# Moving the norm's roots and row scaling of the coming couple to VectorE, inside the visit

## The chip, the cores and the metric

The kernel runs on one core of one Trainium2 chip. The metric is the device time of one execution in microseconds (us), as the median of several runs. A core has several engines that run their own queues of instructions side by side: TensorE (PE in the profile, with PEld for its weight loads), VectorE (DVE), ScalarE (ACT), GpSimd (POOL) and SyncE (SP, which here issues the DMAs). An engine takes its instructions in order: one that waits holds up all that is queued behind it.

## The reference

An attention block with normalised queries and keys feeds a two-layer feed-forward block. In the notation of the reference:

```
q, k, v: (8, 12, 448, 64)      w_in: (768, 2048)      w_out: (2048, 768)
rmsnorm(x, g) = x / sqrt(mean(x*x, axis=-1) + 1e-6) * g
q_n, k_n = rmsnorm(q, g_q), rmsnorm(k, g_k)
attn = softmax(q_n @ k_n^T / 8)
x = (attn @ v).transpose(0, 2, 1, 3).reshape(3584, 768)
h = x @ w_in;  out = (h * sigmoid(h)) @ w_out
```

All inputs and outputs are fp32. The step that the change touches is the norm of the rows of q and k: the mean of the squares of 64 elements, its reciprocal square root, and the multiplication of each row by it.

## The kernel before, in words

The 96 heads are worked off in 24 *couples* of four heads, three couples to a batch. For each couple c the main loop calls `visit(c)` (L1366) and then `between(c)` (L1431). From couple 6 on (GROUP is 6) the rows of q and k lie in a layout of quarters, 32 wide, and are normalised before they are transposed. What the change touches applies from there on.

**The norm of one couple** has these steps.

- `sum_squares` (L649): ScalarE squares the 128x896 rows of q or of k (L654), VectorE sums each 32 of them (L655) into `rms`, 28 columns for q and 28 for k.
- `scale` (L660): TensorE multiplies the sums by a matrix called `ident` (L667), which adds the two halves of a row. The product lands in a tile named "sc". There are two such PSUM buffers, and the tiles of the scores use the same two. VectorE reads the tile (L668) and makes the reciprocal root by a start value and three Newton steps (L672 to L681; small instructions of 128x56). Then GpSimd multiplies the rows by the factors (L689), once for q and once for k, 128x896 each.
- `flip` (L633): VectorE transposes blocks of 32 of q (L636) or k (L639), and the loads of the next rows into the freed place are issued on SP (L251; eight DMAs for each of q and k). `gain` (L643) multiplies the transposed keys by g_q and g_k on ScalarE.

**A visit** (L1366) is TensorE's work on scores and on weighted sums of v in a fixed order: `scores(c, j, i)` (L701) multiplies into one "sc" tile, and ScalarE takes the exponential of it (L715); `weigh` (L725) adds the products with v into two PSUM banks, "av0" and "av1". The last products of couple c−1 are made at the start of visit(c). `turn` (L720) copies one column into such a bank (L723) before TensorE goes on in the other order of halves; in turn(1) this copy is made by VectorE from couple 6 on. When the products of couple c−1 are complete, `divide` (L802) multiplies them by the reciprocal sums on VectorE (L805). In the visits of couples 12 and 18 `sum_x` (L944) follows, with sums of x for the feed-forward products (L828), and in those of couples 7 to 10 sums or roundings of the weights w_in (`weights_in_visit`, L1356). Two or more adds of exponentials (`add`, L752, L761) end the visit.

**Between two visits** (L1431) TensorE works on the feed-forward products x @ w_in. They are made by a scheme of seven products for each 2x2 block (L859 on), of HW = 3 steps of multiplication each per half (six matmul records of a full array, 2.25 us). VectorE adds finished products to earlier ones (L831), ScalarE copies others (L881, L891), and GpSimd adds some (L893). The product tiles use two PSUM buffers named "mm". `fill` (L1305) deals these steps out: it takes steps until the share of this call is used up, calls the entries of `others` spread evenly over these steps, and the entries of `prompt` one at the start and one after each finished product. Each couple has two such calls. The first carries the late adds, the weights' roundings and sums, and the squares of the keys of couple c+2; the second carries the reciprocals of the couple's sums of exponentials in two halves (L790; L781 are TensorE's sums), `gain`, and the squares of the queries of couple c+2. The second half of the reciprocals issues six DMAs on SP that spread them over partitions (`spread`, L796 and L798); `divide` of the next visit needs them. Before the change, `flip` of the queries of c+1 stands at the start of `between`, `flip` of the keys of c+1 between TensorE's last sum and the first reciprocal, and `scale(c + 2)` at the very end of `between(c)`. There are exceptions at the start: the keys of couple 6 are scaled at the end of between(4), behind `pair_up` (L691), which fills `ident` by copies on GpSimd (L695); the queries of couple 6 in visit(5); couple 7 at the start of between(6).

Which of two buffers a tile gets is decided when the program is built. The order of each engine's instructions is the order in which the program issues them.

After couple 23 the remaining feed-forward products (L1180, L1217) follow, from about 778 us to the end. The change does not touch them.

Of the kernel before, what the change touches and what calls it, by code (L numbers as in the profile page):

```python
# [11 lines left out]
F32 = mybir.dt.float32  # L12
AF = mybir.ActivationFunctionType
ALU = mybir.AluOpType
# [15 lines left out]
BANK = 512  # L30
# [487 lines left out]
def bounded(  # L518
# [114 lines left out]
    def flip(c, name):  # L633

        if name == "q":
            nc.vector.transpose(qT.rearrange("p i s -> p (i s)"), q_of(c)[:, 0 : z.NK])  # L636
            load_q(c + 1)
            return
        nc.vector.transpose(kT, place[f"k{c % 2}"])  # L639
        if c + 2 < NC:  # L640
            loads["k"](c + 2)
# [15 lines left out]
            in_=squares.rearrange("p (n e) -> p n e", e=z.Q), axis=AX.X, op=ALU.add,  # L657
        )

    def scale(c, names="qk"):  # L660

        if c >= NC:
            return
        start = "qk".index(names[0]) * n
        f = norm.rms[c % 2][:, ds(start, len(names) * n)]
        t = ps.tile([P, 2, BANK], F32, name="sc", bufs=2)[:, 0, 0 : len(names) * n]
        nc.tensor.matmul(t, ident, f, start=True, stop=True)  # L667
        nc.vector.tensor_scalar(  # L668
            out=f, in0=t, scalar1=1.0 / D, scalar2=1e-6, op0=ALU.mult, op1=ALU.add
        )  # L670
        y, a = (squares[:, ts(i, len(names) * n)] for i in range(2))
        nc.vector.tensor_scalar(  # L672
            out=y.bitcast(I32), in0=f.bitcast(I32), scalar1=-0.5, scalar2=RSQRT_START,
            op0=ALU.mult, op1=ALU.add,
        )
        for i in range(3):
            nc.vector.tensor_tensor(out=a, in0=f, in1=y, op=ALU.mult)
            nc.vector.scalar_tensor_tensor(
                out=a, in0=a, scalar=-0.5, in1=y, op0=ALU.mult, op1=ALU.mult
            )  # L680
            nc.vector.scalar_tensor_tensor(  # L681
                out=f if i == 2 else y, in0=a, scalar=1.5, in1=y, op0=ALU.add, op1=ALU.mult
            )
        for i, name in enumerate(names):
            rows = q_of(c)[:, 0 : z.NK] if name == "q" else place[f"k{c % 2}"]
            rows = rows.rearrange("p (n e) -> p n e", e=z.Q)
            factor = f[:, ts(i, n)]
            factor = factor.rearrange("p (n one) -> p n one", one=1).to_broadcast([P, n, z.Q])
            nc.gpsimd.tensor_tensor(out=rows, in0=rows, in1=factor, op=ALU.mult)  # L689

    def pair_up():  # L691

# [27 lines left out]
    def turn(step, copy):  # L720

        if step != weighed["step"]:
            copy(banks[1][:, S : S + 1], minus_half)  # L723
# [581 lines left out]
    def fill(others=(), prompt=()):  # L1305


        others, prompt, steps, dealt = list(others), list(prompt), 0, 0
        if prompt:
            prompt.pop(0)()  # L1310
        filler["due"] += filler["share"]
        total = max(1, int(filler["due"] / S))
        while filler["due"] > 0:
            step = next(filler["work"], None)
            if step is None:
                break
            filler["due"] -= step
            steps += 1
            if prompt and steps % HW == 0:
                prompt.pop(0)()  # L1320
            while dealt < min(len(others), len(others) * steps // total):
                others[dealt]()
                dealt += 1
        filler["due"] = min(filler["due"], 0.0)
        for other in prompt + others[dealt:]:
            other()
# [24 lines left out]
    def weights_in(c, half):  # L1351
        i = 2 * (c - GROUP) + half
        work = [step_of[step] for step in ("ro" if c < GROUP else halves.get(i, ""))]
        return work + [lambda a=a: sum_w_in(*a) for a in sums_halves.get(i, ())]
# [11 lines left out]
    def visit(c):  # L1366

        if c < GROUP - 1:
            beside = normalise(c + 1)
        elif c <= GROUP:  # L1370
            beside = [lambda: sum_squares(c + 1, "q")]
        else:
            beside = []
        if c < NC:
            scores(c, 0, 0)
        run_all(beside[0:1])
        if c > 0:
            weigh(c - 1, LEFT)
            weigh(c - 1, LEFT - 1, 0)
            turn(1, nc.scalar.copy if c < GROUP else nc.vector.tensor_copy)  # L1380
        if c < NC:
            scores(c, 0, 1)
        if c == 0:
            run_all(beside[1:2])
        if c > 0:
            weigh(c - 1, LEFT - 1, 1)
            if c - 1 < EARLY:
                for i in range(2):
                    nc.vector.tensor_copy(x_of(c - 1, i), sums[i])
                run_all(beside[1:2])  # L1390
                if inverting:
                    if c > 1:
                        divide(c - 2, None)
                    run_all(inverting)
                    inverting.clear()
            else:
                divide(c - 1, sums)
                run_all(beside[1:2])
                if c < NC and c % GROUP == 0:
                    for i in range(0 if c == GROUP else 1, HW):  # L1400
                        sum_x(last_two(c), i)
                weights_in_visit(c)
            if c + 1 < NC:
                loads["vrest"](c + 1)
        if c == NC:
            return
        if c == GROUP - 1:
            scale(c + 1, "q")
        scores(c, 1, 0)
        scores(c, 1, 1)  # L1410
        if c < GROUP:
            run_all(beside[2:3])
        weigh(c, 0, 1)
        scores(c, 2, 0)
        weigh(c, 1, 1)
        turn(0, nc.scalar.copy)
        if c < GROUP:
            run_all(beside[3:4])
        scores(c, 2, 1)
        weigh(c, 0, 0)  # L1420
        run_all(add(c, 1))
        weigh(c, 1, 0)
        scores(c, LEFT)
        if c + 1 < NC:
            loads["v"](c + 1)

    def run_all(work):
        for piece in work:
            piece()

    def between(c):  # L1431

        def transposes_and_sums():
            summing = sum_up(c)
            if c < GROUP:
                next(summing)
            if c == GROUP:
                flip(c + 1, "q")
            if c < GROUP - 1:
                transpose_k(c + 1)  # L1440
            elif c < NC - 1:
                flip(c + 1, "k")
            reciprocals = next(summing)
            if GROUP - 1 <= c < NC - 1:
                reciprocals.insert(2, gain)
            if GROUP // 2 <= c <= EARLY:
                divide(c - 1, None)
            return reciprocals

        if c < GROUP - 1:  # L1450
            transpose_q(c + 1)
        elif c == GROUP:
            scale(c + 1)
        elif c < NC - 1:
            flip(c + 1, "q")
        if c < GROUP // 2:
            inverting.extend(transposes_and_sums())
        elif c == GROUP - 1:
            run_all(transposes_and_sums())
        if c >= GROUP and c % GROUP == 0:  # L1460
            fetched = range(AHEAD) if c == GROUP else ()
            columns = products - 2 * HW * S * len(fetched)
            work = halves_in(last_two(c), range(HF), plain_in, dict(begun), fetched)
            begin(work, columns, 2 * GROUP)
            begun.clear()
        late = add(c, LEFT - 1) + add(c, LEFT) if c >= GROUP else []
        keys = [lambda: sum_squares(c + 2, "k")] if c >= GROUP - 2 else []
        queries = [lambda: sum_squares(c + 2, "q")] if c >= GROUP else []
        fill(late + weights_in(c, 0) + keys)
        prompt = transposes_and_sums() if GROUP // 2 <= c != GROUP - 1 else []  # L1470
        if c == GROUP // 2:
            begin(make_ahead([0, 1]), AHEAD * 2 * HW * S, GROUP - 1)
        fill(weights_in(c, 1), prompt + queries)
        if c == GROUP - 2:
            pair_up()
            scale(c + 2, "k")
        elif c >= GROUP:
            scale(c + 2)
        if c % GROUP == GROUP - 1:
            finish()  # L1480
            if c == GROUP - 1:
                begun[0] = fetch_ahead([0, 1], 0)
            else:
                sum_x([c // GROUP * 2, c // GROUP * 2 + 1], 0)
        if GROUP <= c < NC - 1:

            nc.scalar.activation(first, minus_half, AF.Exp)
        if c == NC - 1:
            while rounder.load():
                pass  # L1490
# [236 lines left out]
```

## Time and profile before

| what | value |
|---|---|
| median of 3 runs | 1362.72 us (1362.27 to 1364.60) |
| the profiled execution | 1364.28 us, of it the span 1362.5 us |
| TensorE's granted clock, mean | 0.989 of full speed |
| ScalarE's exponentials L715 (128x448) | 542 ns each, 252 of them |
| VectorE's reductions L655 | 1082 ns each, 36 of them |
| VectorE's reciprocals L790 | 1533 ns each, 36 of them |
| feed-forward products L873 | 549 ns a matmul record, busy 258.6 + 187.2 us in the two largest groups |

A line of the profile's groups names the source line, the engine, the operation, output and inputs, the shape, how many there were, then the busy time and the mean of one, and at last the engine's idle time just before them with what ended most of it. Busy time of TensorE includes that of instructions that overlap in its pipeline: a matmul record of 549 ns starts every 375 ns when nothing holds it up. In a timeline a line is start, busy time, engine, source line, operation, count; in square brackets stands the idle time before it and what released it.

### The profile page before, as it was taken

To read this page: it belongs to the slowest core of one execution; us is meant where nothing else is said; L and a number is where in the kernel's file an instruction comes from. 1 tells how busy PE (TensorE), PEld (TensorE's weight loads), DVE (VectorE), ACT (ScalarE), POOL (GpSimd) and SP (SyncE) were. 2 spreads that over 40 slices of the span, in tenths; PEclk is the share of its full clock that TensorE was granted. 3 is DMA by queue.
4 is the path that set the end of the run, shared out by engine and by line. 5 is a ranking of instruction groups with operands and counts; after the bars stand their busy time and mean duration, and the time that the engine had idled before them with its cause. 6 is when DMAs were issued, how large, how long until landed. Compare 5 with 4: busy or idle time off the path is not lost.

```text
span 1362.5 us, 19714 instructions
## 1 busy us (share of the span) xinstructions
PE 1302.9 (96%) x7113; PEld 818.6 (60%) x7113; DVE 991.2 (73%) x1785; ACT 475.7 (35%) x859; POOL 266.2 (20%) x205
## 2 busy tenths in 40 slices
PE   8997898999899999899999999999999999999998
PEld 4333343444344444344444455556999999999998
DVE  5786987886756656765664677679887787878786
ACT  7875364464344544444454234420010000000000
POOL 5762223331122122111210134420000000000000
PEclk9999899999999999899999999999999999999999
DMA  8564355334333333233331247531413232323311
GB/s 234 149 151 99 88 147 143 94 75 105 79 78 78 92 92 79 84 78 79 78 92 45 99 134 245 179 118 43 128 50 122 74 97 74 102 78 99 111 60 38
DMA packets 252559, 139.43 MB, mean 102 GB/s; under 512 B 190436, under 2 KB 236388, under 8 KB 252452
## 3 DMA queue, kind: packets, MB, share of 16 engines
q1 hardware_dynamic: 251888, 137.09, 36.1%
q8 instruction: 58, 0.95, 0.3%
q0 software_dynamic: 256, 0.79, 0.2%
q14 instruction: 49, 0.40, 0.1%
q10 hardware_dynamic: 308, 0.20, 0.1%
HBM read 88.47 MB, written 41.29 MB: 95 GB/s over the span
## 4 chain that ended last, share of the span: by engine, by line
PE 64%; DVE 2%; DMA 1%; SPq 1%; ACT 1%; issue 0%; POOL 0%; ACTq 0%; DVEq 0%; POOLq 0%
PE alone L1180 22%; PE mm L873 17%; PE mm L1180 7%; PE alone L873 7%; PE sc L710 4%; PE av L747 4%; PE alone L1217 2%; PE mm L1217 1%; PE sc L781 1%; DVE sums_x L828 0%; DMA hidden<-stage 0%; SPq L251 0%; DVE work L831 0%; DMA work<-work 0%; POOL parts L893 0%
## 5 line engine op out<-in xcount | busy, mean ns | idle before, releaser
L873 PE MATMUL mm<-x,W 128*128 128x448 f32 x636 | 258.6, 549 | 13.8 <-ACT stage L891 5.2
L873 PEld LDWEIGHTS mm<-x,W 128*128 128x128 f32 x636 | 117.6, 191 | 147.5 <-issue 111.9
L873 PE MATMUL mm<-sums_x,W 128*128 128x448 f32 x456 | 187.2, 549 | 7.4 <-DVE stage L831 4.4
L747 PE MATMUL av<-work,rows 64*64 64x448 f32 x1296 | 152.1, 552 | 20.9 <-DVE av L723 15.4
L710 PE MATMUL sc<-work 64*64 64x448 f32 x1344 | 163.7, 558 | 2.2 <-ACT work L715 2.0
L761 DVE TENSOR_TENSOR work<-work 128x896 f32<-128x896 f32 (+1 forms) x114 | 128.6, 1153 | 51.1 <-PE av L747 46.0
L715 ACT ACTIVATE work<-sc 128x448 f32<-128x448 f32 x252 | 120.8, 542 | 95.5 <-PE sc L710 85.6
L873 PEld LDWEIGHTS mm<-sums_x,W 128*128 128x128 f32 x456 | 84.9, 191 | 102.3 <-issue 80.9
L1180 PE MATMUL alone<-W,rows 128*128 128x192 f32 x608 | 113.0, 326 | 0.0
L747 PEld LDWEIGHTS av<-work,rows 64*64 64x64 f32 x1296 | 53.0, 135 | 98.2 <-issue 39.4
L893 POOL TENSOR_TENSOR parts<-parts,stage 128x448 f32<-128x448 f32 x31 | 41.5, 1340 | 318.5 <-DVE parts L831 290.1
L1180 PEld LDWEIGHTS alone<-W,rows 128*128 128x128 f32 x608 | 101.2, 190 | 0.0
L710 PEld LDWEIGHTS sc<-work 64*64 64x64 f32 x1344 | 51.9, 136 | 76.3 <-issue 36.5
L689 POOL TENSOR_TENSOR rows<-rows,rms 128x896 f32<-128x896 f32 x36 | 62.7, 1762 | 143.9 <-ACT work L715 49.2
L505 POOL DMA_DIRECT2D out_dram<-x x2 | 1.3, 652 | 443.1 <-DVE x L831 443.1
L1011 ACT ACTIVATE stage<-stage 128x896 f32<-128x896 f32 x63 | 57.3, 945 | 44.6 <-DVE stage L831 43.9
L1180 PE MATMUL alone<-W,work 128*128 128x192 f32 x382 | 72.2, 326 | 0.0
L1180 PEld LDWEIGHTS alone<-W,work 128*128 128x128 f32 x382 | 63.8, 190 | 0.0
L655 DVE TENSOR_REDUCE rms<-rows 128x28 f32<-128x896 f32 x36 | 38.9, 1082 | 31.8 <-ACT rows L654 31.7
L881 ACT COPY stage<-mm 128x448 f32<-128x448 f32 x27 | 14.3, 531 | 130.2 <-PE mm L873 130.1
L1190 ACT COPY rows<-alone 128x192 f32<-128x192 f32 x34 | 10.8, 318 | 137.5 <-PE alone L1180 79.0
L790 DVE RECIPROCAL work<-sc 128x224 f32<-128x224 f32 x36 | 55.1, 1533 | 1.0 <-PE sc L781 1.0
(248 smaller groups left out, 2168.0 us busy)
## 6 DMA issues: line engine op xcount, KB each, us to landing
hidden<-stage SPq DMA_DIRECT2D x63, 448.0 KB, 2.8
work<-hidden SPq DMA_DIRECT2D x21, 1024.0 KB, 5.2
rows<-in_moe_w_out_dram SPq DMA_DIRECT2D x32, 384.0 KB, 3.4
W<-in_moe_w_in_dram SPq DMA_DIRECT2D x22, 512.0 KB, 5.1
work<-work SPq DMA_DIRECT2D x144, 56.0 KB, 1.9
rows<-in_q_dram SPq DMA_DIRECT2D x144, 56.0 KB, 2.2
rows<-in_k_dram SPq DMA_DIRECT2D x144, 56.0 KB, 2.2
x<-hidden SPq DMA_DIRECT2D x7, 1024.0 KB, 5.6
```

The costliest lines, as they stand in the source:

```text
L655: nc.vector.tensor_reduce(out=norm.rms[c % 2][:, ts("qk".index(name), n)], in_=squares.rearrange("p (n e) -> p n e", e=z.Q), axis=AX.X, op ...
L689: nc.gpsimd.tensor_tensor(out=rows, in0=rows, in1=factor, op=ALU.mult)
L710: nc.tensor.matmul(two[ds(half * D, D), h, 0:S], keys[rows, ts(half, D)], qT[rows, pair, :], start=True, stop=True,)
L715: nc.scalar.activation(eleft[:, h] if j == LEFT else weights(c, j)[:, i, h], two[:, h, 0:S], AF.Exp, scale=norm.column(c, i, h, j) if c < ...
L747: nc.tensor.matmul(sums[i][ds(h * D, D), :], v, w, start=(j == 0 and step == 1), stop=(j == LEFT - 1 and step == 1),)
L761: nc.vector.tensor_tensor(out=total, in0=total, in1=more, op=ALU.add)
L790: nc.vector.reciprocal(out=r[0][:, rows], in_=t[:, rows])
L873: nc.tensor.matmul(t, self.left(name, s), self.right(name, s), start=s == ends[0], stop=s == ends[1])
L893: nc.gpsimd.tensor_tensor(out=u2, in0=u2, in1=p5, op=ALU.add)
L1011: nc.scalar.activation(t, t, AF.Silu)
L1180: nc.tensor.matmul(t, x[:, i], y, start=i == ORDER[0], stop=i == ORDER[-1])
L1217: nc.tensor.matmul(o, a[:, 2 * i + m, t], right_one(name, i)[:, m], start=n == 0, stop=n == len(steps) - 1,)
```

## The change

`scale` loses its choice of names and always does both q and k. The row scaling moves from GpSimd to VectorE (36 instructions of 128x896). It is called for couple c+1 inside visit(c) for c from 5 to 22: behind the loads of v that follow divide (and the sums of `sum_x` or of the weights), ahead of scores(c, 1, 0); at c = 6 behind turn(0), ahead of scores(c, 2, 1). Before, it was called for couple c+2 at the end of `between(c)`, with the exceptions named above.

`flip` of the queries stands at the start of `between` at c = 6 too. `flip` of the keys leaves its place ahead of the first reciprocal and becomes the third `prompt` entry, behind both reciprocals and the spread's DMAs; so the eight loads of keys on SP come behind the spread. `gain` and the squares of the queries go together in a last entry. In the first `fill` the squares of the keys move between the adds, the weights' steps behind all adds, and an empty step is added at the end.

```diff
--- before.py
+++ after.py
@@ -657,18 +657,15 @@
             in_=squares.rearrange("p (n e) -> p n e", e=z.Q), axis=AX.X, op=ALU.add,
         )
 
-    def scale(c, names="qk"):
-
-        if c >= NC:
-            return
-        start = "qk".index(names[0]) * n
-        f = norm.rms[c % 2][:, ds(start, len(names) * n)]
-        t = ps.tile([P, 2, BANK], F32, name="sc", bufs=2)[:, 0, 0 : len(names) * n]
+    def scale(c):
+
+        f = norm.rms[c % 2][:, 0 : 2 * n]
+        t = ps.tile([P, 2, BANK], F32, name="sc", bufs=2)[:, 0, 0 : 2 * n]
         nc.tensor.matmul(t, ident, f, start=True, stop=True)
         nc.vector.tensor_scalar(
             out=f, in0=t, scalar1=1.0 / D, scalar2=1e-6, op0=ALU.mult, op1=ALU.add
         )
-        y, a = (squares[:, ts(i, len(names) * n)] for i in range(2))
+        y, a = (squares[:, ts(i, 2 * n)] for i in range(2))
         nc.vector.tensor_scalar(
             out=y.bitcast(I32), in0=f.bitcast(I32), scalar1=-0.5, scalar2=RSQRT_START,
             op0=ALU.mult, op1=ALU.add,
@@ -681,12 +678,12 @@
             nc.vector.scalar_tensor_tensor(
                 out=f if i == 2 else y, in0=a, scalar=1.5, in1=y, op0=ALU.add, op1=ALU.mult
             )
-        for i, name in enumerate(names):
+        for i, name in enumerate("qk"):
             rows = q_of(c)[:, 0 : z.NK] if name == "q" else place[f"k{c % 2}"]
             rows = rows.rearrange("p (n e) -> p n e", e=z.Q)
             factor = f[:, ts(i, n)]
             factor = factor.rearrange("p (n one) -> p n one", one=1).to_broadcast([P, n, z.Q])
-            nc.gpsimd.tensor_tensor(out=rows, in0=rows, in1=factor, op=ALU.mult)
+            nc.vector.tensor_tensor(out=rows, in0=rows, in1=factor, op=ALU.mult)
 
     def pair_up():
 
@@ -1404,8 +1401,8 @@
                 loads["vrest"](c + 1)
         if c == NC:
             return
-        if c == GROUP - 1:
-            scale(c + 1, "q")
+        if GROUP - 1 <= c < NC - 1 and c != GROUP:
+            scale(c + 1)
         scores(c, 1, 0)
         scores(c, 1, 1)
         if c < GROUP:
@@ -1414,6 +1411,8 @@
         scores(c, 2, 0)
         weigh(c, 1, 1)
         turn(0, nc.scalar.copy)
+        if c == GROUP:
+            scale(c + 1)
         if c < GROUP:
             run_all(beside[3:4])
         scores(c, 2, 1)
@@ -1434,23 +1433,17 @@
             summing = sum_up(c)
             if c < GROUP:
                 next(summing)
-            if c == GROUP:
-                flip(c + 1, "q")
             if c < GROUP - 1:
                 transpose_k(c + 1)
-            elif c < NC - 1:
-                flip(c + 1, "k")
             reciprocals = next(summing)
             if GROUP - 1 <= c < NC - 1:
-                reciprocals.insert(2, gain)
+                reciprocals += [lambda: flip(c + 1, "k"), gain]
             if GROUP // 2 <= c <= EARLY:
                 divide(c - 1, None)
             return reciprocals
 
         if c < GROUP - 1:
             transpose_q(c + 1)
-        elif c == GROUP:
-            scale(c + 1)
         elif c < NC - 1:
             flip(c + 1, "q")
         if c < GROUP // 2:
@@ -1466,16 +1459,13 @@
         late = add(c, LEFT - 1) + add(c, LEFT) if c >= GROUP else []
         keys = [lambda: sum_squares(c + 2, "k")] if c >= GROUP - 2 else []
         queries = [lambda: sum_squares(c + 2, "q")] if c >= GROUP else []
-        fill(late + weights_in(c, 0) + keys)
+        fill(late[:2] + keys + late[2:] + weights_in(c, 0) + [lambda: None])
         prompt = transposes_and_sums() if GROUP // 2 <= c != GROUP - 1 else []
         if c == GROUP // 2:
             begin(make_ahead([0, 1]), AHEAD * 2 * HW * S, GROUP - 1)
-        fill(weights_in(c, 1), prompt + queries)
+        fill(weights_in(c, 1), prompt[:3] + [lambda: run_all(prompt[3:] + queries)])
         if c == GROUP - 2:
             pair_up()
-            scale(c + 2, "k")
-        elif c >= GROUP:
-            scale(c + 2)
         if c % GROUP == GROUP - 1:
             finish()
             if c == GROUP - 1:
```

## The prediction

> **What bounds the kernel now.** I read first the page's busy shares, then the table of busy time over windows of one couple each, then the timeline of TensorE and VectorE in such a window, and the chain of waits last.
>
> ```profile
> PE 1302.9 (96%) x7113; PEld 818.6 (60%) x7113; DVE 991.2 (73%) x1785; ACT 475.7 (35%) x859; POOL 266.2 (20%) x205
> ...
> L747 PE MATMUL av<-work,rows 64*64 64x448 f32 x1296 | 152.1, 552 | 20.9 <-DVE av L723 15.4
> ...
> L689 POOL TENSOR_TENSOR rows<-rows,rms 128x896 f32<-128x896 f32 x36 | 62.7, 1762 | 143.9 <-ACT work L715 49.2
> ```
>
> TensorE is the bound. What is left to win is its idle time, and its largest single cause on the page is a wait for the one-column copy L723. The windows, each from one couple's L723 to the next's (17 to 18, 19 to 20, 21 to 22; columns: us, then busy PE, PEld, DVE, ACT, POOL, the clock, the DMA share, GB/s) say where:
>
> ```profile
> 529.00:570.00 41.00, 34.22 (x188) 15.04 (x182) 26.70 (x39) 19.63 (x33) 12.24 (x8) 0.99 0.34 88
> ...
> 606.00:640.40 34.40, 33.74 (x186) 15.39 (x178) 20.65 (x34) 14.30 (x24) 6.28 (x4) 1.00 0.34 78
> 675.10:708.70 33.60, 33.60 (x186) 15.23 (x178) 20.79 (x34) 17.38 (x28) 5.56 (x4) 1.00 0.33 93
> ```
>
> The window that ends at couple 18's L723 is 6.6 us longer than the next (41.0 against 34.4), with TensorE hardly busier. The one before couple 12 is longer likewise. Their timeline:
>
> ```profile
> 564.55 3.73 POOL L689 TENSOR_TENSOR rows<-rows,rms 128x896 f32<-128x896 f32 x2 [4.61 <-issue]
> 564.78 1.94 DVE L828 TENSOR_TENSOR sums_x<-x 128x448 f32<-128x448 f32 x1
> 566.76 2.00 DVE L828 TENSOR_TENSOR sums_x<-x,sums_x 128x448 f32<-128x448 f32 x1
> 569.75 0.15 DVE L723 COPY av<-minus_half 128x1 f32<-128x1 f32 x1
> ...
> 572.87 0.62 DVE L828 TENSOR_TENSOR sums_x<-x 128x448 f32<-128x448 f32 x1
> ```
>
> L723 stands in VectorE's queue behind the roots and the sums of x. Two of these sums take 1.94 and 2.00 instead of 0.62 us while GpSimd scales rows. A regular visit (couple 21) has no such stall:
>
> ```profile
> 674.87 0.22 DVE L681 SCALAR_TENSOR_TENSOR rms<-rows 128x56 f32<-128x56 f32 x1
> 675.01 0.15 DVE L723 COPY av<-minus_half 128x1 f32<-128x1 f32 x1
> 676.35 1.16 DVE L805 TENSOR_TENSOR x<-av,work 128x448 f32<-128x448 f32 x2 [1.19 <-PE av L747]
> 681.67 2.10 DVE L761 TENSOR_TENSOR work<-work 128x896 f32<-128x896 f32 x2 [4.16 <-PE av L747]
> ```
>
> There the roots end just before L723 is wanted, and VectorE is idle for 4.16 us later in the visit. TensorE's multiplications are packed in slots of 0.375 us (eight records of a half array in about 0.75). What its starts show beyond such slots, I call a stall; between 80 and 778 us these sum to about 60 us. The 585 us after that hold none of the change.
>
> **What the Trainium skill says.** "GPSIMD Engine Reference", section 8, Key points: GpSimd and VectorE contend for the memory path. The trace agrees (1.94 and 2.00 beside 0.62). The same page, 4.1 Engine selection, calls elementwise work about twice as slow on GpSimd; here 1.76 against 1.05 for L761, a factor of 1.7. "VectorE: DVE Perf Modes", in the tier table and the section on the TRN2 errata, leaves a two-tensor fp32 operation without a speed-up: (896 + 151)/0.96 = 1.09 us as an estimate; L761 above has 2.10 for two. "TensorE: Matmul & The Clock Gate", Part 1: the clock falls after idleness and comes back after some 3.4 us of activity. Here the stall of 5.27 us before 569.96 is followed by slots worth another 2.77 us, and the one before 357.63 by 1.45. No page bears on the choice of PSUM buffers.
>
> **The change part by part** (minus is a gain).
>
> *Row scaling on VectorE.* 36 x L689 leave GpSimd (1.76 each) and cost VectorE 1.05 to 1.15 by L761's shape. I take 1.08, so 39 us of VectorE, hidden if it lies in the idle 4.16 us. Bounds: 1.05 and 1.76 (no faster than VectorE's own same shape, no slower than GpSimd). VectorE's excess under L689, operation by operation against its usual time, was 15.2 us in all; it goes. A couple's scale on VectorE is then roots 2.71 + 2.16 = 4.9 us.
>
> *Couples 12 and 18.* Before L723, the roots (2.7) and the contention (2.6 to 2.7) go: nearly all of the stalls of 5.27 and 5.37, and the slow slots behind, 1.45 and 2.77. Whole: 14.9. But scale now follows the sums in the same queue: the score tile that takes over its PSUM buffer waits for L668 behind divide and sums, and three others share the second buffer and wait for each other's exponentials. I charge 3 us each for that, bounds 0 and 5. Net −8.9.
>
> *Couple 5.* Scaling keys in between(4) made TensorE wait for L695's copies:
>
> ```profile
> 106.52 0.41 PE L667 MATMUL sc<-rms,ident 128*128 128x28 f32 x2 [2.69 <-POOL ident L695]
> ```
>
> That wait (2.85 as a stall, 1.7 more in slow slots) goes; 28 more columns of roots and two scalings come in the visit. −3.5, bounds −4.5 and −2.
>
> *Couple 6.* The divide waits 3.72 us for the spread reciprocals, whose DMAs (L796, L798) stand behind eight loads of keys on SP. The change puts them ahead. The roots leave L723's way too (2.81 of stall), but VectorE, the bound of this stretch, gets 2.15 of row scaling. −3 − 2.5 + 2.15, about −3.5; bounds −6 and 0.
>
> *Regular visits, nine couples (13 to 17, 19 to 22).* The new scale takes a score buffer of two. By the built program's buffers, scores(c,1,1) takes it over and so waits for L668, which is behind divide. In couple 21: the last weighing slot begins at 675.70; divide ends near 677.4; L668 takes 0.22 and releases at about 677.7; the buffer is wanted at 677.07 (676.08, two score halves' 0.75, 0.25 of own matmul). 0.62 to 0.67 each: +5.9; bounds 0 (the next weighing absorbs it) and 9. Roots and scaling end 6.5 us after 675.70, the adds are wanted after 6.84: nothing, with 0.34 of slack. If this cover goes, adds, transposes and the first product's copies are late by the excess.
>
> *Block transposes and reciprocals.* Before, flip of k stands between the reduction and the first reciprocal:
>
> ```profile
> 447.07 1.08 DVE L655 TENSOR_REDUCE rms<-rows 128x28 f32<-128x896 f32 x1 [1.57 <-ACT rows L654]
> 448.07 1.10 DVE L639 STREAM_TRANSPOSE work<-rows 128x896 f32<-128x896 f32 x1
> 449.10 1.52 DVE L790 RECIPROCAL work<-sc 128x224 f32<-128x224 f32 x1
> 450.54 0.56 DVE L831 TENSOR_TENSOR parts<-mm,stage 128x448 f32<-128x448 f32 x1
> ```
>
> A product's plus L831 is late by that, and TensorE stalls 0.82 at six couples (13, 14, 16, 17, 19, 20). One operation per product clears it: −4.9, bounds −4.9 and 0. The keys' loads now follow the spread and hidden's DMAs on SP: waits of ScalarE's L891 for hidden cost 1.07 and 0.35 at couples 17 and 20; −1.4. The keys' square is now asked of ScalarE between adds while it does SiLU, and the reduction waits for it in VectorE's queue ahead of L831: I charge 0.3 at nine couples, +2.7 (0 to +6). With +5.9 the regular couples net +2.3.
>
> *Couples 7 to 10.* Between divide and L668 stand four sums of the weights (7 and 9: 3.65 us) or two roundings (8 and 10: about 4.0). The two score tiles after scale share the other buffer, and the second waits about 1.25 us for the first one's exponentials. The third wants scale's buffer 0.375 + 0.25 + 3 x 0.75 + 1.25 = 4.1 us after the last weighing slot's start; L668 comes at 1.71 + 3.65 = 5.36 and releases at 5.64. So 1.25 + 1.5 = 2.8 at 7 and 9, and 3.1 at 8 and 10. Against it, less contention (0.84 to 1.05 each) and parts of old stalls: at 7 and 8 the turns (0.72 and less), at 8 and 10 the clumps of reduction, flip and reciprocal (2.73 and 1.36; 0.92 to 1.81). At 9 the adds are late as well, +0.7. Net: 2.8 − 0.3, 3.1 − 1.4, 2.8 + 0.7, 3.1 − 2.1, sum +8.7; bounds +2 and +14. Couple 11, with a turn's 0.55 and 0.94 before, −0.8.
>
> *Sum.* −8.9 − 3.5 − 3.5 + 2.3 + 8.7 − 0.8 = −5.7 us. The profiled execution took 1364.28 (span 1362.5); the median of the runs is 1362.72, 1.6 less. So 1358.6 profiled and 1357 for the median.
>
> **The rivals.** Measurement tells about 0.2%, 2.7 us.
>
> *Faster, forecast:* 1350 to 1360, chance 0.48.
>
> *Gains given back.* Couples 12 and 18 keep 5 us each of their stalls because the buffer wait replaces the turn (−8.9 becomes −5), and nothing is won at 6: −5.7 + 3.9 + 3.5 = +1.7, so 1364. For: the sums of x stand ahead of L668. Against: GpSimd's contention ends in any case. Chance 0.18 (1360 to 1365.4).
>
> *Slower: the scale chain overruns its idle gap.* If row scaling costs VectorE more than 1.08 + 0.34/2 = 1.25 us, the adds, the flips, and the copies freeing the first products' banks are late in some 17 visits. At 1.76 the lag is 2 x 0.68 − 0.34 = 1.0 us; with the products' VectorE work also pushed, 17 x 1.0 = 17, of which I let 1 to 4 us be absorbed: −5.7 + 15 = +9, so 1372. For: no row I read shows VectorE with this operand, one factor repeated along 32 columns, and the slack is only 0.34. Against: L761's 1.05. Chance 0.31 (1365.4 to 1378).
>
> *Larger gain.* Score waits are absorbed by later slots (−5.9 and half of 8.7): 1347. Chance 0.03.
>
> **How the numbers follow.** Faster 0.48 + 0.03 = 0.51, same 0.18, slower 0.31. The range 1348 to 1374 leaves out most of the last case and a third of the slow one, some 0.13. The forecast's own range is 1350 to 1360.
>
> **What would show it.** Right: no L723 wait over 1 us at couples 12 and 18; L828 back at 0.62; L689 on DVE at 1.05 to 1.15; L790's first reciprocal not behind L639; waits of 0.6 us of scores L710 for L668 in regular visits, 2 to 3 at 7 to 10. Wrong: L689 above 1.25, L761 no longer preceded by idleness, TensorE waiting for L831 or for the first product's copies in regular couples, or L710 never waiting for L668.

## The result, and the profile after

| | before | after |
|---|---|---|
| median of 8 runs each | 1362.34 us (1360.23 to 1364.60) | 1367.69 us (1366.69 to 1369.28) |
| the profiled execution | 1364.28, span 1362.5 | 1367.57, span 1365.7 |

The changed kernel takes 1.0041 times as long (95% interval 1.0030 to 1.0052): 5.4 us more, where 5.7 less were forecast. In the diff `scale` lost three lines, so a line of the kernel after from L664 up to `scale`'s call in the visit stands three lower than its like before: L668 is now L665, L689 is L686, L723 is L720, L831 is L828.

First the shares of the engines and three groups of the page of the kernel after (busy, mean ns; then idle before, and its releaser).

```profile
PE 1308.2 (96%) x7111; PEld 811.8 (59%) x7111; DVE 1017.1 (74%) x1810; ACT 476.5 (35%) x859; POOL 202.3 (15%) x169
...
L707 PE MATMUL sc<-work 64*64 64x448 f32 x1344 | 163.6, 555 | 14.4 <-ACT work L712 10.1
...
L744 PE MATMUL av<-work,rows 64*64 64x448 f32 x1296 | 147.1, 543 | 7.3 <-DVE av L720 4.3
...
L758 DVE TENSOR_TENSOR work<-work 128x896 f32<-128x896 f32 (+1 forms) x114 | 124.0, 1111 | 8.3 <-PE av L744 7.7
```

The idle time ahead of the weighing fell from 20.9 to 7.3 us, the part of it that waits for the turn's copy from 15.4 to 4.3, as forecast. In its place the scores wait 14.4 us instead of 2.2, and the adds, which had 51.1 us of idleness ahead of them, have 8.3. The work went where it was meant to go; the time did not come back.

Where it went is read from the starts of the visits (the first score matmul of a visit in TensorE's timeline), here in differences of the two traces:

| stretch, start to start | before | after | difference | forecast |
|---|---|---|---|---|
| start to visit 4 | 80.58 | 79.44 | −1.1 | 0 |
| couples 4 and 5 | 46.59 | 49.55 | +3.0 | −3.5 |
| couple 6 | 46.64 | 42.87 | −3.8 | −3.5 |
| couples 7 to 10 | 142.12 | 151.32 | +9.2 | +8.7 |
| couple 11 | 33.35 | 32.41 | −0.9 | −0.8 |
| couples 12 and 18 | 81.95 | 72.52 | −9.4 | −8.9 |
| nine regular couples | 307.91 | 313.98 | +6.1 | +2.3 |
| visit 23 to the end | 623.36 | 623.61 | +0.2 | 0 |
| sum | 1362.5 | 1365.7 | +3.2 | −5.7 |

Two rows are wrong, by 6.5 and 3.8 us. The rest of the distance to the 5.4 us of the medians is in the first trace of before, which was 1.9 us above its median.

The gain at couple 18 is seen in the timeline of the visit after:

```profile
567.07 0.62 DVE L825 TENSOR_TENSOR sums_x<-x 128x448 f32<-128x448 f32 x1
567.72 0.63 DVE L825 TENSOR_TENSOR sums_x<-x,sums_x 128x448 f32<-128x448 f32 x1
...
569.33 0.15 DVE L720 COPY av<-minus_half 128x1 f32<-128x1 f32 x1
569.54 0.98 PE L744 MATMUL av<-work,rows 64*64 64x448 f32 x8
```

The sums of x are back at 0.62 us, and the weighing behind L720 shows no wait. A regular visit (couple 21) looks like this:

```profile
675.06 0.93 PE L744 MATMUL av<-work,rows 64*64 64x448 f32 x8
675.92 0.43 PE L664 MATMUL sc<-rms,ident 128*128 128x56 f32 x2
676.36 2.01 PE L707 MATMUL sc<-work 64*64 64x448 f32 x16
677.13 0.21 DVE L665 TENSOR_SCALAR rms<-sc 128x56 f32<-128x56 f32 x1
679.85 2.10 DVE L686 TENSOR_TENSOR rows<-rows,rms 128x896 f32<-128x896 f32 x2
682.27 1.09 DVE L758 TENSOR_TENSOR work<-work 128x896 f32<-128x896 f32 x1 [0.33 <-PE av L744]
```

Row scaling takes 1.05 us an instruction (mean 1.089), and the adds still find VectorE idle for 0.33 us: the slack of 0.34 was read rightly. TensorE, though, goes from the weighing at 675.06 to the scores in 1.30 us where it took 0.75 before, and from the first score tile to the second in 1.03 instead of 0.75.

The two wrong rows show in TensorE's waits for VectorE and, at couple 5, for ScalarE's queue as well. At couple 4:

```profile
96.37 0.42 DVE L124 TENSOR_SCALAR W<-W 128x512 f32<-128x512 f32 x1
97.89 0.95 DVE L825 TENSOR_TENSOR W<-W 128x768 f32<-128x768 f32 x1
98.76 2.24 DVE L802 TENSOR_TENSOR x<-x,work 128x448 f32<-128x448 f32 x2
100.92 1.54 DVE L787 RECIPROCAL work<-mm 128x224 f32<-128x224 f32 x1
102.39 0.56 DVE L828 TENSOR_TENSOR stage<-mm,stage 128x448 f32<-128x448 f32 x1
103.00 3.35 PE L870 MATMUL mm<-x,W 128*128 128x448 f32 x4 [3.89 <-DVE stage L828]
```

A whole rounding of weights and their sum (L124 to L825) now come behind the keys' reduction and just ahead of divide, reciprocal and plus. The product that needs L828's buffer waits 3.89 instead of 1.55 us, and its first slots run slowly (3.35 us for four records). At couple 5 the flip comes late:

```profile
124.67 1.05 DVE L639 STREAM_TRANSPOSE work<-rows 128x896 f32<-128x896 f32 x1
124.90 4.16 PE L870 MATMUL mm<-x,W 128*128 128x448 f32 x6 [2.38 <-DVE work L787]
125.76 1.04 ACT L645 ACTIVATE work<-work,gains 128x896 f32<-128x896 f32 x1 [5.44 <-DVE work L639]
126.71 0.51 ACT L878 COPY stage<-mm 128x448 f32<-128x448 f32 x1
```

The keys' gain L645 waits for the flip, which stands behind both reciprocals, and the copy of a finished product (L878; before the change L881, at 124.15) waits behind the gain. The product at 124.90 does not wait for this copy: by its releaser it has the other buffer, that of the sums which the reciprocals read, and waits 2.38 us for the second of them. Before, the product at this place waited 0.85 us for the copy. And at couple 15, as at 21:

```profile
484.60 1.02 PE L870 MATMUL mm<-x,W 128*128 128x448 f32 x2
484.74 1.56 DVE L787 RECIPROCAL work<-sc 128x224 f32<-128x224 f32 x1 [1.12 <-PE sc L778]
486.33 0.62 DVE L828 TENSOR_TENSOR parts<-mm,parts 128x448 f32<-128x448 f32 x1
487.01 2.52 PE L870 MATMUL mm<-x,W 128*128 128x448 f32 x6 [1.39 <-DVE parts L828]
```

The product whose last records start at 484.60 is added by L828 only behind a reciprocal, and the next product waits for exactly this buffer. That the other one was free is shown by a run below.

### The profile page after: what moved, and what is told of

The parts are those of the page before. It is cut to its first block, busy times and chain, and to the rows that moved or that the text cites. A ratio compares the mean times of both kernels' runs of the same rounds, so it can differ in the third digit from the quotient of the medians.

```text
span 1365.7 us, 19617 instructions
## 1 busy us (share of the span) xinstructions
PE 1308.2 (96%) x7111; PEld 811.8 (59%) x7111; DVE 1017.1 (74%) x1810; ACT 476.5 (35%) x859; POOL 202.3 (15%) x169
## 4 chain that ended last, share of the span: by engine, by line
PE 50%; DVE 1%; issue 0%; ACT 0%; ACTq 0%; DVEq 0%
PE alone L1177 22%; PE mm L870 8%; PE mm L1177 7%; PE alone L870 7%; PE alone L1214 2%; PE av L744 1%; PE sc L707 1%; PE mm L1214 1%; DVE work L828 0%; PE sc L778 0%; DVE x L828 0%; DVE x L802 0%; DVE rows L825 0%; DVE sums_x L825 0%; DVE work L787 0%
## 5 line engine op out<-in xcount | busy, mean ns | idle before, releaser
L707 PE MATMUL sc<-work 64*64 64x448 f32 x1344 | 163.6, 555 | 14.4 <-ACT work L712 10.1
L744 PE MATMUL av<-work,rows 64*64 64x448 f32 x1296 | 147.1, 543 | 7.3 <-DVE av L720 4.3
L758 DVE TENSOR_TENSOR work<-work 128x896 f32<-128x896 f32 (+1 forms) x114 | 124.0, 1111 | 8.3 <-PE av L744 7.7
L707 PEld LDWEIGHTS sc<-work 64*64 64x64 f32 x1344 | 46.8, 134 | 97.5 <-issue 31.4
L1187 ACT COPY rows<-alone 128x192 f32<-128x192 f32 x34 | 10.8, 318 | 137.5 <-PE alone L1177 79.0
L870 PE MATMUL alone<-x,W 128*128 128x448 f32 x132 | 53.7, 551 | 1.4 <-DVE x L802 1.4
L1191 ACT COPY rows<-alone 128x192 f32<-128x192 f32 x34 | 10.8, 319 | 123.1 <-PE alone L1177 119.6
```

The costliest lines, as they stand in the source:

```text
L707: nc.tensor.matmul(two[ds(half * D, D), h, 0:S], keys[rows, ts(half, D)], qT[rows, pair, :], start=True, stop=True,)
L744: nc.tensor.matmul(sums[i][ds(h * D, D), :], v, w, start=(j == 0 and step == 1), stop=(j == LEFT - 1 and step == 1),)
L758: nc.vector.tensor_tensor(out=total, in0=total, in1=more, op=ALU.add)
L870: nc.tensor.matmul(t, self.left(name, s), self.right(name, s), start=s == ends[0], stop=s == ends[1])
L1187: nc.scalar.copy(p1, product(1))
```

## The experiments

Ratios are to the kernel before, from runs of both on one chip, with 95% intervals. The changed kernel has 1.0041.

**Scale's tile out of the scores' buffers.**

```diff
-        t = ps.tile([P, 2, BANK], F32, name="sc", bufs=2)[:, 0, 0 : 2 * n]
+        t = bank(2 * n)
```

> The changed kernel, with one edit: the PSUM tile of scale comes from the two buffers of the feed-forward products, which stand idle in a visit, and no longer from the two of the scores. Theory (score tiles wait for L668 because scale holds one of their two buffers): the waits of scores in the visits of couples 7 to 10, 12 and 18 (2 to 3.5 us each in the trace of the changed kernel) and 0.78 us in each of nine regular couples go, about 20 us in all; some 1347 to 1352 us. Rival (VectorE is too full; its chain of roots, scaling and adds is the bound): the wait moves from the scores to the adds and the first products, and at most 5 us are won, 1363 or more.

Measured: 1364.01 us, ratio 1.0011 [1.0003, 1.0018], 3.7 us less than the change. The rival was right. The waits of the scores (2.3 to 2.7 us at couples 7 to 9) are gone, but in all of couples 7 to 10 a product some 17 us into the couple waits 2.6 to 3.6 us instead, here at couple 9:

```profile
261.94 2.09 DVE L686 TENSOR_TENSOR rows<-rows,rms 128x896 f32<-128x896 f32 x2
263.95 2.08 DVE L758 TENSOR_TENSOR work<-work 128x896 f32<-128x896 f32 x2
265.95 1.10 DVE L636 STREAM_TRANSPOSE work<-rows 128x896 f32<-128x896 f32 x1
266.98 0.58 DVE L828 TENSOR_TENSOR stage<-mm,stage 128x448 f32<-128x448 f32 x1
267.62 2.61 PE L870 MATMUL mm<-sums_x,W 128*128 128x448 f32 x3 [3.40 <-DVE stage L828]
```

VectorE works without a gap through scaling, adds and flip, and the product waits for its plus. (At 8 and 10 it waits for a copy of ScalarE, which had waited 6.12 us for VectorE's adds.) At couples 7 and 9 this product starts 17.13 us into the couple, and with the change 17.14: up to there VectorE is the bound, and the wait for a score buffer only stood in front of it. In a regular couple the edit wins 0.36 to 0.42 us. At couple 21 the first score tile comes 0.08 us earlier in the visit and the weighing behind the second 0.36, which is all that holding a score buffer is worth; this weighing is still 0.52 us later in the visit than before the change.

**The old order up to couple 5.**

```diff
-        fill(late[:2] + keys + late[2:] + weights_in(c, 0) + [lambda: None])
+        if c < GROUP:
+            fill(weights_in(c, 0) + keys)
+        else:
+            fill(late[:2] + keys + late[2:] + weights_in(c, 0) + [lambda: None])
...
+            elif c == GROUP - 1:
+                flip(c + 1, "k")
             reciprocals = next(summing)
...
-                reciprocals += [lambda: flip(c + 1, "k"), gain]
+                reciprocals += [gain] if c == GROUP - 1 else [lambda: flip(c + 1, "k"), gain]
```

> The changed kernel, with the order of before in the steps up to couple 5: the weights' rounding ahead of the keys' squares in between(4) and before, and in between(5) the flip of the keys ahead of the reciprocals. Theory (the loss at couple 5 comes from this order, which the change moves for the early couples too): the stalls of 4.05 at 103 us and 2.55 at 125 us shrink to 1.7 and 0.9 with the slow slots behind them, so about 5 to 7 us less than the changed kernel, near 1362. Rival (the two row scalings put into visit 5 fill VectorE): about 1 us less, 1366 to 1367.

Measured: 1363.63 us, ratio 1.0005 [0.9994, 1.0015], 4.1 us less than the change, where 5 to 7 were expected. In its trace, of an execution 4.3 us above this median, the two waits are back at about what they were:

```profile
102.07 1.40 PE L870 MATMUL mm<-x,W 128*128 128x448 f32 x3 [1.82 <-DVE stage L828]
...
120.14 2.52 PE L870 MATMUL mm<-x,W 128*128 128x448 f32 x6 [0.86 <-ACT stage L878]
```

The turn of couple 6 comes 6.3 us earlier than with the change. But the flip that goes back ahead of the reciprocals takes its eight loads of keys with it, ahead of the spread on SP, and the divide of visit 6 waits for the spread again:

```profile
122.10 4.09 SPq L251 DMA_DIRECT2D rows<-in_k_dram  x8
126.61 2.61 SPq L793 DMA_DIRECT2D work<-work  x4
134.28 1.15 DVE L802 TENSOR_TENSOR x<-av,work 128x448 f32<-128x448 f32 x2 [5.71 <-DMA work<-work]
```

With the change the spread comes first, and the divide waits for TensorE alone:

```profile
124.98 2.47 SPq L793 DMA_DIRECT2D work<-work  x4
129.84 3.98 SPq L251 DMA_DIRECT2D rows<-in_k_dram  x8
136.80 1.16 DVE L802 TENSOR_TENSOR x<-av,work 128x448 f32<-128x448 f32 x2 [1.89 <-PE av L744]
```

Of the 6.3 us, 2.5 are left at the divide and 2.3 at the next turn; couple 8 gives back 1.5 more. The divide follows the turn after 3.8 to 5.9 us in all eight traces with the old order at couple 5 (both of the kernel before among them) and after 1.3 to 2.1 in the six with the new one. So the order that costs at couple 5 is also the one that pays at couple 6. A kernel with the flip ahead of the reciprocals and its loads behind the spread was not run. Visit 5 itself, with its row scalings on VectorE, was not the loss.

**The products' buffers strictly in turn.**

```diff
-            return ps_mm.tile([P, BANK], F32, name="mm")[:, 0:n]
+            alternate["next"] = 1 - alternate["next"]
+            return ps_mm.tile([P, BANK], F32, name=f"mm{alternate['next']}", bufs=1)[:, 0:n]
```

> The changed kernel, with the two buffers of the feed-forward products taken strictly in turn (two names of one buffer each). Theory (a product after couples 8, 15 and 21 gets the buffer of the product just before it and so waits for the plus behind the reciprocal): stalls of 3.0, 1.55 and 1.58 go, 5 to 6 us less, near 1362. Rival (the plus behind the reciprocal is late whichever buffer is taken): no change, 1367 to 1368.

Measured: 1361.12 us, ratio 0.9995 [0.9985, 1.0006], 6.6 us less than the change. At couple 15:

```profile
483.96 3.27 PE L872 MATMUL mm<-x,W 128*128 128x448 f32 x8
484.10 1.56 DVE L787 RECIPROCAL work<-sc 128x224 f32<-128x224 f32 x1 [1.12 <-PE sc L778]
485.69 0.62 DVE L828 TENSOR_TENSOR parts<-mm,parts 128x448 f32<-128x448 f32 x1
487.07 2.42 PE L872 MATMUL mm<-sums_x,W 128*128 128x448 f32 x6
```

The reciprocal and the plus are no earlier, yet TensorE runs through: the buffer and not the order made this wait. Couples 15 and 21 become 1.7 us shorter each and couple 8 1.3. Couples 4 and 5 become 3.5 us longer in this trace, as the product of couple 5 now waits 4.75 us for the late copy (L880 here), and couple 6 gives 3.2 of it back.

**Row scaling back on GpSimd, in the new place.**

```diff
-            nc.vector.tensor_tensor(out=rows, in0=rows, in1=factor, op=ALU.mult)
+            nc.gpsimd.tensor_tensor(out=rows, in0=rows, in1=factor, op=ALU.mult)
```

> The changed kernel, with the row scaling L686 back on GpSimd, in its new place. Theory (VectorE is not the bound in the visits, the order of waits is): VectorE loses 39 us of work and nothing is won; adds and sums slow down beside GpSimd again: 1367 to 1373. Rival (VectorE too full): 5 us or more are won, 1363 or less.

Measured: 1375.35 us, ratio 1.0096 [1.0080, 1.0112], 7.7 us more than the change and a little more than expected. VectorE has 38 us less to do, but its 78 adds of 128x896 run beside GpSimd:

```profile
L758 DVE TENSOR_TENSOR work<-work 128x896 f32<-128x896 f32 x78 | 107.7, 1412 | 31.2 <-PE av L744 31.1
```

1412 ns each instead of 1101 with the change, 24 us in all. In the new place VectorE is the better engine for this work.

**The new order alone, and the new place alone.** The first puts `scale` back where it was (for couples from 7 on, on GpSimd) and keeps the order; the second keeps the place and VectorE and puts the order of `between` back. The main lines of the first:

```diff
-        if GROUP - 1 <= c < NC - 1 and c != GROUP:
+        if c == GROUP - 1:
             scale(c + 1)
...
-        if c == GROUP:
-            scale(c + 1)
...
+        elif GROUP <= c < NC - 2:
+            scale(c + 2)
```

> The changed kernel with scale put back for couples from 7 on (end of between(c) for couple c+2, start of between(6) for couple 7) and its row scaling back on GpSimd; the new order of reciprocals, flip of the keys, squares and weights stays, and so does scale of couple 6 in visit 5. Theory (the new order costs 3 us at couples 4 and 5 and 1.6 at each of couples 15 and 21, and saves 0.8 at six couples and about 1 at the DMA waits): +0 to +5 us on the kernel before, 1362 to 1367, and the stalls at couples 12 and 18 of over 5 us are there. Rival (the order is a gain and the place of scale is the loss): 3 to 6 us less than the kernel before, 1356 to 1359.

> The changed kernel with the order of before in between (keys' flip ahead of the reciprocals, gain third, keys' squares behind the weights); scale stays inside the visit and on VectorE. Theory (the place gives 9.4 us at couples 12 and 18 and takes 0.62 us in each regular visit and about 9 us at couples 7 to 10): +2 to +6 us on the kernel before, 1364 to 1368. Rival (the whole loss comes from the order): 0 to 4 us less than the kernel before.

Measured: the order alone 1357.46 us, ratio 0.9958 [0.9944, 0.9973]; the place alone 1371.59 us, ratio 1.0063 [1.0046, 1.0080]. The order is a gain of 5 us in spite of its loss at couples 4 and 5: there the rival was right. For the place alone both expectations were too low (2 to 6 us more, or 0 to 4 less). The new place, with its engine, loses 10.2 us on top of the new order and 8.9 us on top of the old. In the traces, turn to turn, it costs 13.6 us in couples 7 to 10 and 0.7 to 0.8 in each of seven regular couples (0.2 and 1.1 at 18 and 22) and gains 4.3 ahead of each of couples 12 and 18. In the order alone, the old wait at couple 18 is there again:

```profile
561.00 2.00 DVE L825 TENSOR_TENSOR sums_x<-x,sums_x 128x448 f32<-128x448 f32 x1
...
564.19 1.77 PE L744 MATMUL av<-work,rows 64*64 64x448 f32 x8 [5.20 <-DVE av L720]
```

**The first three edits together.** Scale's tile takes the products' buffer that was not used last, without taking a turn.

> The changed kernel with the three edits of the first runs together: scale's PSUM tile from the products' buffers, the old order up to couple 5, the products' buffers strictly in turn. If their gains (3.7, 4.1 and 6.6 us by the medians) add up: 1353 to 1355 us. If they pay for the same stalls of VectorE at couples 6 to 10: 1357 to 1360.

Measured: 1356.85 us, ratio 0.9952 [0.9936, 0.9969]. The gains don't add up (14.4 us by the three medians, 10.8 measured); what takes up the rest is not shown. This kernel is 5.9 us faster than the one before: with the two failing places mended and scale's tile moved, the change gives about what the sum had forecast.

**Scale's matmul at the end of between.** This starts from the three edits together; `squares_joined` holds the matmul L664 alone, into the products' buffer that was not used last.

```diff
+        if GROUP < c + 1 < NC - 1:
+            squares_joined(c + 2)
         if GROUP <= c < NC - 1:
...
-        nc.tensor.matmul(t, ident, f, start=True, stop=True)
+        t = summed_at[c]
```

> As the run with the three edits together, and scale's matmul L664 stands at the end of between, behind full-array products, as before the change; what VectorE does of scale stays inside the visit. Theory (in the visit, between half-array multiplications, this matmul takes about 0.5 us of TensorE, at the end of between 0.16): 0.3 to 0.4 us less in each of 16 visits, 5 to 6 us less than that run. Rival (the 0.5 us is a wait of the scores and not the matmul's place): no change against that run.

Measured: 1362.44 us, ratio 0.9998 [0.9987, 1.0009], 5.6 us more than the run before it. Neither holds. With the starts of both traces laid side by side, the first score tile behind this place comes 0.47 us earlier in a regular visit (couple 21), as the theory had it. But the matmul now needs a buffer whose last product isn't copied yet, ahead of visit 17 for instance:

```profile
527.30 0.53 ACT L900 COPY stage<-mm 128x448 f32<-128x448 f32 x1 [4.48 <-DMA hidden<-stage]
...
527.89 0.43 PE L664 MATMUL mm<-rms,ident 128*128 128x56 f32 x2 [1.59 <-ACT stage L900]
```

ScalarE's copy waits for a DMA, TensorE for the copy. At the ends of couples 16 and 19 the matmul starts 1.75 and 1.33 us late, at those of 13, 15 and 21 0.2 to 0.4; at 14, 17 and 20 it is on time, and products earlier in the couple are late by some tenths. In sum the nine regular couples are 3.2 us longer.

**The kernel before once more.**

> The kernel before, unchanged, for a second trace of it. If its first profiled execution (1364.28 us, 1.9 above the median) was longer by slow slots of TensorE behind stalls at some couples, the second differs there alone and by 1 to 3 us; the waits of 5.3 us at couples 12 and 18 and of 0.82 us at six couples are the same in both.

Measured: 1367.31 us in this one execution, span 1365.4; runs beside it had a median of 1362.47. Turn to turn, the couples 13 to 16 and 19 to 22 agree with the first trace within 0.03 us, and 12, 17 and 18 within 0.3. Couple 6 differs by 0.7, couple 8 by 1.9, the stretch up to the turn of couple 6 by 1.1 and the one behind the last turn by 1.7. Behind stalls TensorE's slots run at half speed for a while: the clock granted in the trace is then 0.50, from 133.1 us on for 10.2 us in this trace, from 138.9 on for 3.4 in the first. So a difference of 0.2 us at couples 13 to 16 and 19 to 22 is a finding, and one of 1 to 2 us up to couple 8 is not. Against this second trace the table's rows for couples 4 and 5, for 6 and for 7 to 10 are +3.8, −3.6 and +6.5.

**The new order, old place, old order up to 5, buffers in turn; and with scale in visits 12 and 18 alone.** The first joins edits shown above. The second adds (scale takes its engine as an argument there, GpSimd unless VectorE is named):

```diff
-        if c == GROUP - 1:
-            scale(c + 1)
+        if c == GROUP - 1 or c in (2 * GROUP, 3 * GROUP):
+            scale(c + 1, nc.vector)
...
-        elif GROUP <= c < NC - 2:
+        elif GROUP <= c < NC - 2 and c + 1 not in (2 * GROUP, 3 * GROUP):
             scale(c + 2)
```

> As the run of the new order alone (scale in its old place and on GpSimd), with the old order up to couple 5 and the products' buffers strictly in turn. Theory (each of these losses has its own place and no other work takes it over): 4 us at couples 4 and 5 and 1.4 at each of couples 15 and 21 less than that run, 1349 to 1352 us. Rival (the early gain is used up at couple 6, where VectorE is the bound): 1353 to 1356.

> As the run before it, and in the visits of couples 12 and 18 alone scale is called for the next couple as in the changed kernel, on VectorE behind the sums of x, instead of at the end of the couple before. Theory (only there does the new place pay): 4.3 us less at each, 8 to 9 us less than that run, 1341 to 1344 us. Rival (scale's lateness is paid in the following couple): 0 to 3 us less.

Measured: 1354.40 us, ratio 0.9936 [0.9919, 0.9953], where the rival was right in that couple 6 uses up part (4.2 of 6.2 us, of which 2.1 by the divide's wait for the spread); and 1343.32 us, ratio 0.9864 [0.9846, 0.9882]. Two calls of `scale` moved into two visits win 11.1 us. In the traces it is 5.3 and 5.4 us ahead of couples 12 and 18, of which couple 18 gives back 1.4; couple 8, where the edit does nothing, differs by 2.0. This kernel is 19 us faster than the one before and 24 faster than the change.

**VectorE in the old place.** The new order alone with the one line of L686 back on VectorE.

> As the run of the new order alone (scale at the end of the couple before), but with the row scaling on VectorE. Theory (in the old place scale stands ahead of the turn's copy in VectorE's queue, and the roots alone already end just in time): the copy is 2.1 us late in some 15 visits, 25 to 32 us more than that run, about 1383 to 1390 us; the waits at couples 12 and 18 are as long as before, since the contention that goes is as large as the scaling that comes. Rival (VectorE has room there too): 0 to 5 us more, up to 1362.

Measured: 1397.63 us, ratio 1.0259 [1.0236, 1.0281], 40 us more than the order alone, and more than I worked out. A regular visit (couple 16):

```profile
513.24 2.09 DVE L686 TENSOR_TENSOR rows<-rows,rms 128x896 f32<-128x896 f32 x2
515.25 0.15 DVE L720 COPY av<-minus_half 128x1 f32<-128x1 f32 x1
515.46 0.98 PE L744 MATMUL av<-work,rows 64*64 64x448 f32 x8 [1.88 <-DVE av L720]
```

Against the order alone, TensorE's wait costs 2.1 to 2.2 us at couples 13, 14 and 16, about its own length, but 3.9 at 15, 19, 20 and 21, where slots at half speed follow it. Between 80 and 775 us the granted clock is at 0.50 for 58.0 us in this trace, against 23.9 for the order alone: some 17 us of the 40, as an estimate from half of the difference.

With the order the same, the four corners are then: old place on GpSimd 1357.5, old place on VectorE 1397.6, new place on GpSimd 1375.4, new place on VectorE 1367.7. Each half of the move is bad without the other, and both together are still behind leaving it.

## Why the prediction was wrong

*Couple 5, the step that failed most.* I priced what leaves (a wait for L695's copies, 2.85 and 1.7 us) and found nothing in its place; I did not follow the rest of the edit back into `between(4)` and `between(5)`. The weights' steps move to the end of the list for every couple, and there put a rounding ahead of divide and plus; at couple 5, where nothing is dealt out over products, "third prompt" means behind both reciprocals at once, with gain and a product's copy behind. The product got the buffer that the reciprocals read. −3.5 was +3.0 for couples 4 and 5, and putting that order back brought 4.1 us. The wait that I had priced did go: in the six traces with the old order and the new place of couple 6's scale, the two couples are 2.7 to 5.0 us shorter than before.

*Couple 6.* −3.8 against −3.5, but one of its two gains was misread. The divide's wait for the spread went, as forecast. The 2.81 us of stall that I put down to roots did not: ahead of L723 VectorE has roundings of weights and reductions there, and no roots. Before, then after:

```profile
133.05 0.98 PE L747 MATMUL av<-work,rows 64*64 64x448 f32 x8 [2.65 <-DVE av L723]
134.97 1.71 PE L744 MATMUL av<-work,rows 64*64 64x448 f32 x8 [2.74 <-DVE av L720]
```

So the size is in part luck, and the gain goes when the order that costs at couple 5 is put back: in the same six traces couple 6 differs from before by −0.8 to +0.3.

*The regular couples.* In "Block transposes and reciprocals" the term "I charge 0.3 at nine couples" was mis-sized as the whole cost of the new order. The stall of 0.82 went at six couples as forecast (at 14, 17 and 20 it had ended with the copy L891 and not with L831), and the charge came at the same six, with 0.33 to 0.40. But couples 15 and 21 lost 1.55 and 1.58 to a product that was given the buffer of the one before, where they had lost 0.15. I had taken the built program's buffers for the scores and not for the products. The visit's own term was about right in size, 0.7 to 0.9 at nine couples against 0.62 to 0.67, and wrong in its mechanism, so that its size was luck. At couple 21 the weighing behind the two score tiles is 0.88 us later in the visit. Of this the score buffer accounts for 0.36; the other 0.52 is TensorE's own time for L664 between half-array multiplications, where it had taken 0.16 at the end of `between`; so 0.72 in all. In sum: visits +6.8 for +5.9, the charge +2.2 for +2.7, couples 15 and 21 +2.8 with no term, the stalls and the DMA waits −6.4 for −6.3, and 0.7 in small pieces.

*Right.* Couples 12 and 18 (−9.4 against −8.9) and, within the spread of the two traces of before, the size for 7 to 10 (+9.2 against +8.7). For 7 to 10 the mechanism was only half right: the score tiles do wait, but freeing their buffer won little, since VectorE is the bound there. The price of row scaling (1.089 against 1.08) and the slack (0.33 against 0.34) held, so the slower rival that I had written down, an overrun in 17 visits, is not what made it slower. The slowdown had another mechanism, which stood in none of my cases: an order that was changed for all couples and costs at the two where its surroundings differ, and a choice of buffer (shown by the runs that put back the order and the turns). I gave slower 0.31 on a wrong ground.

*The base.* I summed from one trace of before that was 1.9 us above its median, part of it slow slots at couples 5 and 6 that I booked as gains.

What stays open: why couples 6 to 8 take up an earlier gain only in part, beyond the divide's wait for the spread (stretches at half clock behind stalls change from trace to trace there), and how much of the 13.6 us of place at couples 7 to 10 is roots and how much is row scaling.

## What to carry to other kernels

Follow every moved line into each call that reaches it, the special cases first: the gain was worked out for the typical couple, and the loss sat in the two that are not. Where tiles come from a pool of two buffers, read which buffer each tile gets in the built program, for every user of every pool; one repeated buffer made TensorE wait for work that two buffers would have hidden. And move an operation only where a measured wait is: moved into two visits it won 11 us, moved into eighteen it lost 10, each against the same kernel with the operation in its old place (2.5 once the early order, the buffers' turns and scale's tile were mended: 1356.85 against 1354.40).

## What the runs showed of the hardware

The pair of 128x56 matmuls over the full array (L664) costs TensorE 0.16 us behind full-array products and about 0.5 us between multiplications of half arrays. That its place decides is shown by moving it (the first score tile comes 0.47 us earlier in the visit); why is not. With the row scaling on GpSimd inside the visit VectorE's adds took 1412 ns on average, with it on VectorE 1101; the sums of x took up to 2.00 us beside row scaling on GpSimd and 0.62 without.

A stall can cost more than its own length. In the last run TensorE waited about 2.2 us at each of the couples 13, 14, 19, 20 and 21; at 13 and 14 this cost 2.2 us, at 19 to 21 3.9, because slots of 0.375 us then took 0.75. From 477.9 to 481.2 us, at couple 15, the granted clock in that trace is 0.50, and 1.00 ahead of it and behind. In the traces' records of this clock each such stretch is 3.41 us long, or two or three times that, in all traces of this case between 80 and 775 us. Which stall is followed by one differs between executions of the same kernel, and the mean clock of 0.977 in that run, against 0.991 for the order alone, reflects them.
